# P·V of the last two token tiles from float16 halves: splitting softmax weights and v, with the subtraction shared by VectorE and GpSimd

## The chip, the cores and the metric

The kernel runs on one core of a Trainium2 chip. The metric is the device time of one execution in microseconds (us); lower is better. The core has a matrix engine (TensorE, PE in the profile, with its weight loads listed apart as PEld), VectorE (DVE), ScalarE (ACT), GpSimd (POOL) and SyncE (SP), which issues most DMAs. Each engine works through its own queue in the order in which the program stands there, and waits on semaphores of the others. PSUM, where matmul results land, is short here: two one-bank tiles for dense products (m0, m1), two two-bank tiles for scores (s) and one two-bank tile (po).

## The reference

The input x is 2048 tokens of 512 numbers. The output is x + s * g: s is sliding-window attention over a layer-normed x, g a gated feed-forward branch of x that goes through one more SiLU.

```python
H = 32; Dh = D // H; W = 256                                   # D = 512, so Dh = 16
qkv = (x @ wqkv).reshape(B, S, 3, H, Dh).transpose(2, 0, 3, 1, 4)
scores = jnp.einsum("bhqd,bhkd->bhqk", q, k) * (Dh ** -0.5)
mask = (idx[:, None] - idx[None, :] >= 0) & (idx[:, None] - idx[None, :] < W)
p = softmax(where(mask, scores, -1e9)); o = jnp.einsum("bhqk,bhkd->bhqd", p, v)   # then @ wo
gate = x @ w1; up = x @ w3; h = silu(gate) * up; out = h @ w2                    # F = 1792
xn = layernorm(x); s = A(xn, wqkv, wo); g = silu(B(xn, w1, w3, w2)); return x + s * g
```

All is float32 in the reference. A query sees itself and the 255 keys before it.

## The kernel before

**Halves.** Nearly every product is float32 made of float16 halves: a number a is split into hi = float16(a) and lo = float16(a - hi), and three matmuls hi·hi, hi·lo and lo·hi are summed in PSUM. ScalarE usually writes hi and VectorE or GpSimd writes lo as a subtraction. One product is not split: the softmax weights times v (called P·V here) is a float32 matmul.

**Units.** Tokens come in four tiles of 512 (t = 0 to 3) and heads in four groups of eight (g). A unit is a pair of heads in each half of the group (p = 0, 1), so there are 32 units, numbered n = 8t + 2g + p. A unit has a first pass (`pass1`, L653: row maxima of the scores, which VectorE takes at L685) that runs two units ahead, and a second pass (`pass2`, L738): scores again, transposed, with the maximum subtracted (L759), masks added on VectorE (L766), exponential on ScalarE into a float32 tile pt of 128x1024 (L769), and then P·V (L787).

The second pass of a unit is cut into five chunks c0 to c4 of scores for t > 0 (`CHUNKS`). Chunk c0 is for both heads a; c1 and c3 are for a = 0, c2 and c4 for a = 1. P·V takes 48 matmuls per unit: the array is used as eight tiles of 64 rows by 32 columns, so eight matmuls (two row halves h, four heads) run side by side. `values` (L773) puts them in six such groups of eight: the first is of c0, the next two of c1 and c2, the last three of c3 and c4. The columns that one array tile takes in the six groups are 256, 320, 192, 320, 128 and 64 (or 64 and 128): 1280 in all. V holds 16 columns of v and a column of ones for each head, so that the sum of the weights comes out of the same matmul.

**Order.** The PE queue is in the order of the text (`ORDERED`); on the other engines a scheduler decides, and work under `urgent()` goes ahead. A unit's work on PE is written as five batches (`PLAN`, in `batches`) with dense matmuls between them (`spread`): W stands for a chunk of scores, M, X and N for a piece of the first pass of the unit after next, and the last batch holds P·V. Before, c0, c1 and c2 come in the first three batches and c3 with c4 in the fourth; the first pass of the last batch is 16 narrow matmuls (48 rows by 32 columns), right ahead of P·V. The last two units, which have no first pass beside them, go by `LAST_PLANS` with four batches.

**Dense work** between the batches is the feed-forward branch (`gate_up`, L1055; `folds`, L1198, a seven-product scheme for the down projection at t > 1), the projections (`project`, L601, and `value`, L567) and the output product (`total`, L1332). For t > 1, VectorE's product at L1079 makes one 128x512 float32 tile h of the feed-forward branch. Two such tiles make the operands of the folded product: `fold_first` (L1115, four operations on GpSimd, L1121 to L1113) after the first, `fold_second` (L1127, eleven, L1136 to L1113) after the second. `turn_beside` (L504) transposes the normed x of a later token tile beside the scores; it costs VectorE two copies of 128x256 for each piece (L524, L525).

**Buffers.** pt tiles are five float32 buffers. Other temporary tiles are taken from 54 slots of 2 KB per partition (`take`, `give`).

## Time and profile before

| | |
|---|---|
| median of three runs | 804.23 us (804.05 to 804.49) |
| the profiled execution | 803.54 us, of which its span on the core is 801.4 us |
| busy: PE, DVE, ACT, POOL | 791.6, 620.4, 395.5, 387.6 us |
| P·V on PE (L787) | 77.2 us in 2880 instructions |
| granted clock of PE | full |

A float32 matmul stands in the trace as two matmuls and two weight loads, so the 1440 matmuls of P·V are 2880 rows. A busy PE has its pipeline filled; a row's duration has the time through the array in it, so that starts, and not durations, tell the rate. "Idle before" is time in which the engine had nothing running. The times of the views that follow are counted from the start of the span.

### The profile page before, as it was taken

How to read it: one execution, taken by the hardware profiler on the slowest of the kernel's cores; microseconds unless marked ns; L12 is line 12 of the kernel's file. 1: busy time of each engine (PE TensorE's matmuls, PEld its weight loads, DVE VectorE, ACT ScalarE, POOL GpSimd, SP SyncE). 2: the span in 40 equal slices, each digit the busy share in tenths (PEclk: the TensorE clock that was granted, in tenths of full speed). 3: DMA queues.
4: the chain of work that ended last, by engine and by line, in shares of the span. 5: the costliest groups of instructions: out<-in, count | busy, mean ns of one | idle time of the engine just before them, and what ended most of it. 6: DMA issues, size and time to landing. Idle time of an engine off the chain costs nothing.

```text
span 801.4 us, 23995 instructions
## 1 busy us (share of the span) xinstructions
PE 791.6 (99%) x9181; PEld 404.0 (50%) x9181; DVE 620.4 (77%) x2001; ACT 395.5 (49%) x596; POOL 387.6 (48%) x762
## 2 busy tenths in 40 slices
PE   9999999999999999999999999999999999999997
PEld 4444445444454444444445444466544744467465
DVE  8886889778798678787888887776678876874537
ACT  6989777744355544344443344344434334444411
POOL 2357657633329436365443546330446276650770
PEclk9999999999999999999999999999999999999999
DMA  9887655636666564657556743656553553343431
GB/s 284 239 260 239 202 185 145 242 111 193 189 216 187 168 212 139 212 156 255 142 191 171 209 115 101 180 169 159 140 158 90 156 161 106 89 121 127 133 89 60
DMA packets 109858, 134.18 MB, mean 167 GB/s; under 512 B 18928, under 2 KB 64944, under 8 KB 109744
## 3 DMA queue, kind: packets, MB, share of 16 engines
q1 hardware_dynamic: 109456, 132.13, 55.4%
q8 instruction: 72, 1.18, 0.7%
q10 hardware_dynamic: 288, 0.52, 0.2%
q14 instruction: 42, 0.34, 0.1%
HBM read 91.23 MB, written 36.57 MB: 159 GB/s over the span
## 4 chain that ended last, share of the span: by engine, by line
PE 81%; DVE 6%; DMA 5%; ACT 3%; SPq 3%; issue 1%; POOL 1%; DVEq 0%; ACTq 0%; POOLq 0%
PE m L1055 31%; PE po L787 9%; PE m L601 8%; PE m L1198 8%; PE m L1280 7%; PE s L759 5%; PE m L1332 4%; PE m L567 4%; PE s L671 3%; DMA slot<-in_B_w_dram 2%; PE po L671 2%; DVE junk L685 1%; POOL slot L345 1%; DMA KA<-dK 1%; SPq L880 1%
## 5 line engine op out<-in xcount | busy, mean ns | idle before, releaser
L1055 PE MATMUL m<-XH,slot 128*128 128x512 f16 x896 | 267.3, 380 | 0.8 <-DVE slot L1074 0.4
L769 ACT ACTIVATE pt<-s,es 128x1024 f32<-128x1024 f32 x152 | 167.6, 1113 | 175.9 <-DVE s L766 168.8
L1055 PEld LDWEIGHTS <-slot 128*128 128x128 f16 x1344 | 124.8, 98 | 155.2 <-issue 12.6
L1055 PE MATMUL m<-XL,slot 128*128 128x512 f16 x448 | 169.8, 379 | 0.0
L766 DVE TENSOR_TENSOR s<-s,MK 128x256 f32<-128x256 f32 (+2 forms) x280 | 118.8, 434 | 54.5 <-PE s L759 50.0
L685 DVE CUSTOM_DVE_ANT_0 junk<-s,MW 128x320 bf16<-128x320 f32 x276 | 133.9, 485 | 19.8 <-PE s L671 11.3
L339 POOL TENSOR_TENSOR slot<-slot,slot 128x256 f16<-128x256 f32 (+1 forms) x86 | 57.6, 693 | 121.4 <-DVE slot L1336 54.7
L345 POOL TENSOR_TENSOR slot<-slot,slot 128x128 f16<-128x128 f32 x184 | 74.9, 441 | 77.8 <-ACT slot L343 51.3
L685 DVE CUSTOM_DVE_ANT_0 junk<-po,MW 128x320 bf16<-128x320 f32 x172 | 83.4, 485 | 4.6
L1280 PE MATMUL m<-slot,slot 128*128 128x512 f16 x336 | 78.5, 380 | 1.4 <-DVE slot L1074 1.4
L787 PE MATMUL po<-pt,V 64*32 64x320 f32 (+4 forms) x2880 | 77.2, 342 | 0.1
L601 PE MATMUL m<-XH,slot 128*128 128x512 f16 x240 | 70.8, 380 | 0.5 <-DVE slot L1074 0.5
L1198 PE MATMUL m<-slot,slot 128*128 128x256 f16 x588 | 68.4, 273 | 0.0
L1070 ACT ACTIVATE slot<-m,sgs 128x512 f32<-128x512 f32 x56 | 38.3, 685 | 60.4 <-PE m L1055 60.3
L1113 POOL TENSOR_TENSOR slot<-slot,slot 128x256 f16<-128x256 f32 x98 | 64.6, 671 | 1.1
L1198 PEld LDWEIGHTS <-slot 128*128 128x128 f16 x588 | 56.2, 98 | 11.4 <-issue 2.8
L787 PEld LDWEIGHTS po<-pt,V 64*32 64x32 f32 x2880 | 50.5, 106 | 22.4 <-issue 0.8
L1074 DVE SCALAR_TENSOR_TENSOR slot<-slot,m 128x512 f32<-128x512 f32 x56 | 38.3, 684 | 28.4 <-ACT slot L1070 27.9
L759 PE MATMUL s<-qa,KA 50*64 50x320 f16 (+3 forms) x1472 | 58.3, 259 | 0.0
L601 PEld LDWEIGHTS <-slot 128*128 128x128 f16 x392 | 36.5, 98 | 42.6 <-issue 1.8
L759 PEld LDWEIGHTS <-KA 50*64 50x64 f16 x1472 | 30.1, 105 | 51.7 <-issue 31.5
L1280 PEld LDWEIGHTS <-slot 128*128 128x128 f16 x336 | 30.8, 98 | 39.5 <-issue 5.1
(194 smaller groups left out, 1132.6 us busy)
## 6 DMA issues: line engine op xcount, KB each, us to landing
slot<-dW SPq DMA_DIRECT2D x98, 256.0 KB
slot<-in_B_w_dram SPq DMA_DIRECT2D x56, 256.0 KB
slot<-dFold SPq DMA_DIRECT2D x48, 256.0 KB
dW<-slot SPq DMA_DIRECT2D x42, 256.0 KB
slot<-in_A_x_dram SPq DMA_DIRECT2D x30, 256.0 KB
KA<-dK SPq DMA_DIRECT2D x24, 288.0 KB
slot<-dWQ SPq DMA_DIRECT2D x24, 256.0 KB
qa<-dQ SPq DMA_DIRECT2D x30, 192.0 KB
```

Source lines behind the costliest of these rows:

```text
L339: op(out[:, c], a[:, c], b[:, c])
L345: nc.gpsimd.tensor_sub(lo[:, c:c + P], raw[:, c:c + P], hi[:, c:c + P])
L601: nc.tensor.matmul(cell["pp"][:, cols[n]], w[:, (a * NC + c) * P:(a * NC + c + 1) * P], b[:, c, cols[n]], start=n == 0 and (c, i) == parts ...
L685: lasts["maximum"] = nc.vector.tensor_tensor_reduce(out=junk[:, :n], in0=s[:, r, :n], in1=mask, scale=1.0, scalar=NEG, op0=ALU.add, op1=AL ...
L759: nc.tensor.matmul(s[64 * h:64 * h + 64, r, o:o + 64 * n], ka[rows, 2 * p + a, 64 * (m + 4):64 * (m + 5)], qa[rows, 2 * p + a, 64 * (m + k ...
L766: nc.vector.tensor_add(v, v, MK[:, kind, of:of + n, :].unsqueeze(1).to_broadcast([P, 2 * len(which), n, 64]))
L769: lasts["exp"] = nc.scalar.activation(pt, s, AF.Exp, scale=es)
L787: nc.tensor.matmul(cell["po"][32 * i:32 * i + 32, h, 64 * (m + k):64 * (m + k + n)], V[64 * h:64 * h + 64, (4 * t + m // 2) % VB, hd * VW: ...
L1055: nc.tensor.matmul(cell[k], w[:, (a * NC + c) * P:(a * NC + c + 1) * P], b[:, c, :], start=c == 0 and i == 0, stop=c == NC - 1 and i == 2)
L1113: nc.gpsimd.tensor_sub(lo, view, hi)
L1198: nc.tensor.matmul(cell["ps"][:, c], made[:, f:f + P], wj[:, g:g + 256], start=j == j0 and c == 0 and n == 0, stop=j == j1 - 1 and n == 2, ...
L1280: nc.tensor.matmul(ps, hh[:, a * TW + b * P:a * TW + (b + 1) * P], w[:, c * D:(c + 1) * D], start=f == f0 and i == 0, stop=f == f1 - 1 and ...
```

## The change

Four things, in neutral words:

1. For t > 1 (units 16 to 31) P·V is made of three float16 matmuls in place of one float32 matmul: hi of v times hi of p, lo of v times hi of p, hi of v times lo of p, group by group, each pass of eight matmuls after the other (L825). After the exponential, ScalarE copies pt to float16 (L801), and lo = pt - hi is made in three pieces: columns 512 to 1023 on VectorE (L802) and two of 256 on GpSimd (L804). The float32 pt tile has two buffers by turns there; hi and lo of c0 and c1 lie in slots, those of c2, c3 and c4 in one buffer each.
2. v comes as float16 halves for blocks 8 to 15: hi by ScalarE, lo by VectorE (L586), with four small memsets on GpSimd each. Blocks 6 and 7 are split on their own (`part_values`) in unit 13. v is scaled by a constant now, where before a number worked out from the weights was used; two small VectorE operations on that number go away.
3. For units 16 to 29 the batches are dealt out differently (`PARTED_PLAN`): c0 and c1 share the first batch and c2, c3 and c4 have a batch each, with two pieces of the first pass beside each of them. `parted` lets finishing a maximum and `turn_beside` follow each other in neighbouring pieces.
4. `measure` for feed-forward blocks 4 and 5 (t = 0) has two of its four squares on VectorE instead of ScalarE. The output product of the very last block goes in column parts of 256, 128 and 128 instead of 256 and 256.

```diff
@@ value
-            if half:
+            if not half:
+                return
+            by_head = lambda v: v[:, 0:H * VW].rearrange("p (h w) -> p h w", w=VW)
+            pv = pv.rearrange("p (h d) -> p h d", d=DH)
+            s = VS / (WS * XS)
+            if j < 8:
                 with urgent():
-                    nc.scalar.activation(V[:, j % VB, 0:H * VW].rearrange(...)[:, :, 0:DH], pv.rearrange(...), AF.Copy, scale=sc["uv"])
+                    nc.scalar.activation(by_head(V[:, j % VB, :])[:, :, 0:DH], pv, AF.Copy, scale=s)
+                return
+            both = V[:, j % VB, :].bitcast(F16)
+            VF[j] = hi, lo = both[:, 0:VR], both[:, VR:]
+            with urgent():
+                nc.scalar.activation(by_head(hi)[:, :, 0:DH], pv, AF.Copy, scale=s)
+                lasts["emptied"] = nc.vector.scalar_tensor_tensor(by_head(lo)[:, :, 0:DH], pv, s, by_head(hi)[:, :, 0:DH],
+                                                                  op0=ALU.mult, op1=ALU.subtract)
+            for v, one in ((hi, VS / OS), (lo, 0.0)):
+                nc.gpsimd.memset(by_head(v)[:, :, DH], one)
+                nc.gpsimd.memset(v[:, H * VW:], 0.0)
@@ pass1
-            elif alone[0] and maxima and (ii, a) != (0, 0):
+            elif alone[0] and maxima and (parted[0] or (ii, a) != (0, 0)):
...
-            alone[0] = not after or t * NG + g <= 2
+            alone[0] = not after or t * NG + g <= 2 or parted[0]
@@ pass2, scores
-            cell[c] = pt = ppool.tile([P, 2, 512], F32, name="pt")
+            pt = ppool.tile([P, 2, 512], F32, name="pt", tag=f"pt{c % 2 if t > 1 else in_pt[0] % 5}", bufs=1)
             with urgent():
                 lasts["exp"] = nc.scalar.activation(pt, s, AF.Exp, scale=es)
+            if t < 2:
+                cell[c] = pt
+                return
+            if c < 2:
+                cell[c] = hi, lo = [take(F16) for _ in range(2)]
+            else:
+                both = ppool.tile([P, 2048], F16, name="pt", tag=f"pt{c}", bufs=1)
+                cell[c] = hi, lo = both[:, 0:1024], both[:, 1024:]
+            pt = pt.rearrange("p r q -> p (r q)")
+            with urgent():
+                lasts["exp"] = nc.scalar.copy(hi, pt)
+                nc.vector.tensor_sub(lo[:, 512:], pt[:, 512:], hi[:, 512:])
+                for q in (0, 256):
+                    nc.gpsimd.tensor_sub(lo[:, q:q + 256], pt[:, q:q + 256], hi[:, q:q + 256])
@@ pass2, values
+            groups = list(zip_longest(*(turns[k] for k in sorted(turns))))
+            if t > 1:
+                for group in groups:
+                    for kv, kp in ((0, 0), (1, 0), (0, 1)):
+                        for c, o, h, a, (m, k, n, _, _) in filter(None, group):
+                            for r in range(2):
+                                ...
+                                nc.tensor.matmul(cell["po"][32 * i:32 * i + 32, h, 64 * (m + k):64 * (m + k + n)],
+                                                 VF[4 * t + m // 2][kv][64 * h:64 * h + 64, hd * VW:hd * VW + 32],
+                                                 cell[c][kp][64 * h:64 * h + 64, 512 * r + o:512 * r + o + 64 * n], ...)
+                give(*cell[0], *cell[1], after=2)
+                return
@@ measure
-        sb = squares([...], on_act=4 if f > 2 else 2, apart=apart)
+        sb = squares([...], on_act=4 if f > 4 else 2, apart=apart)
@@ total_by_columns
-        for c in (slice(0, 256), slice(256, 512)):
-            ps = bank([P, 256])
+        for c in (slice(0, 256), slice(256, 384), slice(384, 512)):
+            ps = bank([P, c.stop - c.start])
@@ plans
     PLAN = (("WM", ()), ("WMX", ()), ("WMX", ()), ("WWX", ()), ("NN", (0, 1, 2, 3, 4)))
+    PARTED_PLAN = (("WW", ()), ("WMX", ()), ("WMX", ()), ("WMX", ()), ("NN", (0, 1, 2, 3, 4)))
-        plan = AHEAD_PLAN if not u else LAST_PLANS[n - len(units) + 2] if not ahead else PLAN if u[0] else FIRST_PLAN
+        plan = AHEAD_PLAN if not u else LAST_PLANS[n - len(units) + 2] if not ahead else (FIRST_PLAN, PLAN, PARTED_PLAN, PARTED_PLAN)[u[0]]
@@ part_values (new)
+        for j in (6, 7):
+            VF[j] = hi, lo = [take(F16) for _ in range(2)]
+            with behind_exp():
+                nc.scalar.copy(hi[:, 0:VR], V[:, j, :])
+            for c in range(0, VR, 256):
+                cols = slice(c, min(c + 256, VR))
+                nc.gpsimd.tensor_sub(lo[:, cols], V[:, j, cols], hi[:, cols])
```

How the queues move is shown at three places.

On PE, the end of unit 18: the last of the narrow matmuls of the first pass and the start of P·V. Before, eight float32 matmuls of one group are one row each, and no weight load stands apart:

```order
L671 LDWEIGHTS qa
L671 MATMUL s<-KA_141,qa 32x320
L787 MATMUL po<-pt,V 32x256 x8
L787 MATMUL po<-pt,V 32x320 x8
L787 MATMUL po<-pt,V 32x192 x8
L787 MATMUL po<-pt,V 32x320 x8
L787 MATMUL po<-pt,V 32x128 x4
L787 MATMUL po<-pt,V 32x64 x8
L787 MATMUL po<-pt,V 32x128 x4
```

In the changed kernel the first group of the same unit reads (V and slot_6329 are the halves of v, slot_8544 and slot_8545 hi and lo of c0; each kind stands several times):

```order
L690 LDWEIGHTS qa
L690 MATMUL s<-KA_141,qa 32x320
L825 LDWEIGHTS V
L825 MATMUL po<-slot_8544,V 32x256
L825 LDWEIGHTS slot_6329
L825 MATMUL po<-slot_8544,slot_6329 32x256
L825 LDWEIGHTS V
L825 MATMUL po<-slot_8545,V 32x256
L825 LDWEIGHTS V
L825 MATMUL po<-slot_8563,V 32x320
```

48 instructions have become 144 matmuls with a weight load each, and the lo half of a chunk is read in the third pass of a group.

On GpSimd, unit 31. Before, `fold_first` of one pair of tiles and `fold_second` of it follow each other:

```order
L1121 TENSOR_TENSOR slot_13235<-slot_13214 128x256
L1112 CAST slot_13234<-slot_13235 128x256
L1113 TENSOR_TENSOR slot_13234<-slot_13214,slot_13234 128x256
L1113 TENSOR_TENSOR slot_13234<-slot_13235,slot_13234 128x256
L1136 TENSOR_TENSOR slot_13311<-slot_13214,slot_13289 128x256
L1137 TENSOR_TENSOR slot_13311<-slot_13311,slot_13214 128x256
L1113 TENSOR_TENSOR slot_13315<-slot_13289,slot_13315 128x256
L1138 TENSOR_TENSOR slot_13235<-slot_13289,slot_13311 128x256
L1113 TENSOR_TENSOR slot_13315<-slot_13289,slot_13315 128x256
L1112 CAST slot_13344<-slot_13311 128x256 x2
L1113 TENSOR_TENSOR slot_13344<-slot_13311,slot_13344 128x256 x2
L1112 CAST slot_13224<-slot_13235 128x256
```

In the changed kernel the same pair, from the last operations of `fold_first` on (L804 x4 is lo of c2 and c3, the last row lo of c4):

```order
L1164 TENSOR_TENSOR slot_15139<-slot_15140,slot_15139 128x256
L804 TENSOR_TENSOR pt<-pt 128x256 x4
L1187 TENSOR_TENSOR slot_15226<-slot_15119,slot_15204 128x256
L1188 TENSOR_TENSOR slot_15226<-slot_15226,slot_15119 128x256
L1164 TENSOR_TENSOR slot_15230<-slot_15204,slot_15230 128x256
L1189 TENSOR_TENSOR slot_15140<-slot_15204,slot_15226 128x256
L1163 CAST slot_15264<-slot_15226 128x256 x2
L1164 TENSOR_TENSOR slot_15264<-slot_15226,slot_15264 128x256 x2
L1163 CAST slot_15129<-slot_15140 128x256
L1164 TENSOR_TENSOR slot_15129<-slot_15140,slot_15129 128x256
L804 TENSOR_TENSOR pt<-pt 128x256 x2
```

Lo of c2 and c3 stands between the two, and lo of c4 behind the whole of `fold_second`. The same order (all of `fold_second`, then lo of c4) is found in units 17 and 26; in unit 28 seven of the eleven operations stand ahead of it.

On VectorE, unit 16, the third batch (c3 in the changed kernel). Before:

```order
L766 TENSOR_TENSOR s<-s,MK 128x2x2x64
L685 ISA junk,M<-s,MW 128x320
L524 CAST XH<-s 128x2x128
L685 ISA junk,M<-po,MW 128x320
L525 TENSOR_TENSOR XL<-s,XH 128x2x128
L1079 SCALAR_TENSOR_TENSOR slot_7555<-m_7606,slot_7555 128x512
```

Now:

```order
L785 TENSOR_TENSOR s<-s,MK 128x2x2x64
L704 ISA junk,M<-s,MW 128x320
L529 CAST XH<-s 128x2x128
L704 ISA junk,M<-po,MW 128x320
L530 TENSOR_TENSOR XL<-s,XH 128x2x128
L802 TENSOR_TENSOR pt<-pt 128x512
L529 CAST XH<-po 128x2x128
L1130 SCALAR_TENSOR_TENSOR slot_7616<-m_7684,slot_7616 128x512
L530 TENSOR_TENSOR XL<-po,XH 128x2x128
```

A subtraction of the softmax weights and a second piece of `turn_beside` have come in. Over the whole unit VectorE has ten copies of `turn_beside` (L529, L530) where it had four, over unit 17 six as before, and over unit 18 none where it had six.

More of the change, by code (lines that the diff above doesn't have):

```diff
@@ L781, in values @@
                         turns.setdefault(item[1:3], []).append((c, *item))
-            for group in zip_longest(*(turns[k] for k in sorted(turns))):
+            groups = list(zip_longest(*(turns[k] for k in sorted(turns))))
[4 more added lines that the diff above has]
+                            for r in range(2):
+                                i = 2 * r + a
+                                hd = g * 8 + r * 4 + 2 * p + a
+                                nc.tensor.matmul(cell["po"][32 * i:32 * i + 32, h, 64 * (m + k):64 * (m + k + n)],
+                                                 VF[4 * t + m // 2][kv][64 * h:64 * h + 64, hd * VW:hd * VW + 32],
+                                                 cell[c][kp][64 * h:64 * h + 64, 512 * r + o:512 * r + o + 64 * n],
+                                                 start=(h, i) not in begun, stop=c == len(chunks) - 1 and kp == 1,
+                                                 skip_group_check=True)
+                                begun.add((h, i))
+                give(*cell[0], *cell[1], after=2)
+                return
+            for group in groups:
                 for c, o, h, a, (m, k, n, _, _) in filter(None, group):
@@ L1492, in batch @@
                 alone[0] = True
+                parted[0] = bool(u) and u[0] > 1
                 for f in rows:
@@ L1652, in tile_block @@
             second()
+        if n == 13:
+            later(2, part_values)
         if n == 6:
@@ L1657, in tile_block @@
             beside_scores(12, lambda s: then(s, wout[2](s), lambda: later(2, lambda: wout[3](2)), lambda: later(3, out_scale)))
+        if n == 24:
+            later(1, lambda: give(*VF.pop(6), *VF.pop(7)))
         want += a_unit - other[n]
```

18 lines of the change are left out of this document (11 added, 7 removed).

## The prediction

> **What bounds the kernel now.** I read the page's head first, then its chain of waits and its groups of instructions.
>
> ```profile
> PE 791.6 (99%) x9181; PEld 404.0 (50%) x9181; DVE 620.4 (77%) x2001; ACT 395.5 (49%) x596; POOL 387.6 (48%) x762
> PE 81%; DVE 6%; DMA 5%; ACT 3%; SPq 3%; issue 1%; POOL 1%; DVEq 0%; ACTq 0%; POOLq 0%
> L787 PE MATMUL po<-pt,V 64*32 64x320 f32 (+4 forms) x2880 | 77.2, 342 | 0.1
> ```
>
> TensorE is busy 99% of the span and carries 81% of the chain that ended last; ahead of P·V (L787) it idled 0.1 us in the whole run. Time is therefore saved only where the PE queue gets shorter, and any new wait in that queue is paid in full, because nothing idle stands behind it to give it back. A row's duration has the way through the array in it, so I take starts from PE's timeline; these are around one P·V, and one dense stretch of the chain.
>
> ```profile
> 562.55 0.64 PE L759 MATMUL s<-qa,KA 50*64 50x320 f16 x24
> 563.02 0.31 PE L671 MATMUL po<-KA,qa 48*64 48x320 f16 x4
> 567.28 0.47 PE L671 MATMUL s<-KA,qa 48*32 48x320 f16 x16
> 567.56 2.53 PE L787 MATMUL po<-pt,V 64*32 64x256 f32 x96
> 570.03 0.60 PE L1055 MATMUL m<-XH,slot 128*128 128x512 f16 x2
> 448.02 3.99 PE m L1055 x18
> ```
>
> P·V of a unit occupies 570.03 - 567.56 = 2.47 us. The dense stretch gives the streaming rate: 3.99 us / (18 x 512) = 0.43 ns per column.
>
> **P·V on PE.** An array tile takes 1280 columns. Two rows per float32 matmul at 2.47 us fit four passes over them: 4 x 1280 x 0.43 = 2.20 us, and some 0.3 us of change-over (2.17 with the unrounded rate). Three float16 passes stream in 1.63 us; with the same 0.3 a unit takes 1.92, a gain of 0.55 us, over 16 units **-8.8 us**. The bounds: with the change-over mostly gone 1.74 us, -11.6 in all. On the other side, what may count is not columns but pairs of load and matmul: there are 144 now against 96. The trace has 24 pairs in 563.02 - 562.55 = 0.47 us (19.6 ns each) and 16 in 567.56 - 567.28 = 0.28 (17.5). 144 at 19.6 ns are 2.82 us, +0.35 a unit, **+5.7** in all. I take the streaming end: both those stretches carry enough columns to be at the streaming rate themselves (16 x 320 over eight tiles x 0.43 = 0.28), so they are no evidence of a floor per pair.
>
> The Trainium skill, "TensorE: Matmul & The Clock Gate", section "Wait — 56ns, not 53.3ns?", says that starts never come closer than about 25 ns however small the matmul is. By that rule 144 would take 3.6 us and the change would lose some 18 us on PE alone, an estimate from that page. The trace disagrees with it for matmuls on separate array tiles: 17.5 ns.
>
> **The new work beside it.** 80 chunks pass through it, five in each of 16 units. Durations by kind, from the groups kept apart by shape:
>
> ```profile
> L769 ACT ACTIVATE pt<-s,es 128x1024 f32<-128x1024 f32 x152 | 167.6, 1113 | 175.9 <-DVE s L766 168.8 <-DVE M L685 3.0 <-PE m L1280 2.3
> L343 ACT CAST slot<-slot 128x512 f16<-128x512 f32 x46 | 27.4, 610 | 0.5
> L1110 ACT CAST slot<-slot 128x256 f16<-128x256 f32 x42 | 15.6, 403 | 59.8 <-DVE slot L1079 59.8
> L766 DVE TENSOR_TENSOR s<-s,MK 128x256 f32<-128x256 f32 x224 | 92.9, 427 | 54.1 <-PE s L759 49.8 <-ACT slot L1088 1.4 <-PE s L711 0.9
> L1338 DVE TENSOR_TENSOR slot<-slot,slot 128x512 f32<-128x512 f32 x3 | 2.0, 683 | 0.0
> L524 DVE CAST XH<-s 128x256 f16<-128x256 f32 x17 | 7.1, 420 | 0.0
> L1113 POOL TENSOR_TENSOR slot<-slot,slot 128x256 f16<-128x256 f32 x98 | 64.6, 671 | 1.1
> ```
>
> ScalarE's copy of 1024 columns: 256 more cost 207 ns, so 610 + 2 x 207 = 1.03 us. VectorE's subtraction 0.68, GpSimd's two 1.30 to 1.34. A unit gains 5.2 us on ScalarE, 3.4 on VectorE, 6.6 on GpSimd, in a period of some 23 us. On average there is room on all three; what decides is the place in the queue. The halves of v (eight short VectorE operations, and `part_values` in unit 13) fall where ScalarE and GpSimd have room; I cost them at nothing beyond VectorE's share below.
>
> When is c4 wanted? Take T4 as the start of its scores on PE. Ahead of P·V stand c4's scores (0.24), two pieces of the first pass (0.3), 18 dense matmuls (3.99) and the 16 narrow ones (0.28): P·V starts at T4 + 4.8. The first lo of c4 is read behind the first three groups and two passes of the fourth: (3 x 768 + 2 x 320) columns x 0.43 = 1.25 us later, at **T4 + 6.1**. It is ready after 0.24 of scores, two masks (0.87), the exponential (1.11), the copy (1.03), some 0.25 of hand-overs, so hi at T4 + 3.5, and 1.3 on GpSimd: **T4 + 4.8**. The spare is 1.3 us in a unit in which GpSimd is free. It is not free where `fold_second` stands ahead of c4's lo in its queue, as in units 17, 26, 31 and for seven of eleven operations 28. GpSimd and PE there:
>
> ```profile
> 451.56 0.73 POOL L1136 TENSOR_TENSOR slot<-slot,slot 128x256 f32<-128x256 f32 x1 [8.92 <-DVE slot L1079]
> 458.03 0.73 POOL L1121 TENSOR_TENSOR slot<-slot 128x256 f32<-128x256 f32 x1
> 451.94 0.64 PE L759 MATMUL s<-qa,KA 50*64 50x320 f16 x24
> ...
> 652.43 0.73 POOL L1136 TENSOR_TENSOR slot<-slot,slot 128x256 f32<-128x256 f32 x1 [4.09 <-DVE slot L1079]
> 651.55 0.64 PE L759 MATMUL s<-qa,KA 50*64 50x320 f16 x24
> ...
> 698.00 0.73 POOL L1136 TENSOR_TENSOR slot<-slot,slot 128x256 f32<-128x256 f32 x1 [3.25 <-DVE slot L1079]
> 696.67 0.64 PE L759 MATMUL s<-qa,KA 50*64 50x320 f16 x24
> ...
> 748.77 0.73 POOL L1136 TENSOR_TENSOR slot<-slot,slot 128x256 f32<-128x256 f32 x1
> 756.38 1.30 POOL L1113 TENSOR_TENSOR slot<-slot,slot 128x256 f16<-128x256 f32 x2
> 760.43 0.73 POOL L1136 TENSOR_TENSOR slot<-slot,slot 128x256 f32<-128x256 f32 x1 [2.75 <-DVE slot L1079]
> 765.19 2.55 PE L787 MATMUL po<-pt,V 64*32 64x256 f32 x96
> ```
>
> `fold_second` lasts 458.03 - 451.56 = 6.47 us and starts when VectorE's second product lands. Unit 17: start near T4 (it was 0.4 before; c3's lo now stands ahead), so c4's lo is done at T4 + 0.1 + 6.5 + 1.3 = 7.9, **+1.8**. Unit 26: product at 652.43 = T4 + 0.9, lo at T4 + 8.65, **+2.5**. Unit 28: T4 + 1.3, 4.6 us of it ahead, lo at T4 + 7.2, a wait of 1.1; with lo of the earlier chunks still in the queue up to 3.1; I take **+2**. Unit 31: GpSimd had the previous `fold_second` and a `fold_first` from 748.77 to 757.68. With 2.6 us for lo of c0 and c1 these end at 760.3, with c2 and c3 at 762.9, then `fold_second` to 769.4, c4's lo at 770.7. P·V, 0.55 us shorter in each unit alike, would want it at 765.19 - 0.55 + 1.25 = 765.9: **+4.8**. Together **+11.1**. Behind the waiting matmul everything on PE waits.
>
> **The common price of VectorE and GpSimd.** A VectorE subtraction with both inputs in SBUF is new here at this density. The opening shows such a meeting:
>
> ```profile
> L345 POOL TENSOR_TENSOR slot<-slot,slot x184: 416/428/907, 31.7 to 245.9; 128x128 f16<-128x128 f32 x184
> 31.69 2.42 POOL L345 TENSOR_TENSOR slot<-slot,slot 128x128 f16<-128x128 f32 x5 [26.40 <-DMA dQ<-slot]
> 31.84 0.82 DVE L251 CUSTOM_DVE_ANT_0 junk<-slot 128x512 bf16<-128x512 f32 x1
> L251 DVE CUSTOM_DVE_ANT_0 junk<-slot 128x512 bf16<-128x512 f32 x10 | 7.0, 698 | 0.1
> ```
>
> GpSimd's subtractions range from 0.43 to 0.91 us, the first five take 2.42 where 5 x 0.43 = 2.14 were due, and VectorE's square beside them 0.82 instead of 0.70. So an overlap costs up to 0.48 us on GpSimd. In ordinary units the spare of 1.3 us covers it; in the four units above it is paid, 4 x 0.5 = **+2**. The Trainium skill, "SBUF — State Buffer", section "Who interferes with whom", calls this an exclusive lock in which the later operation waits out the whole earlier one. By it the four units pay 0.7 each, an estimate; the row shows less.
>
> **VectorE near its limit.** Stretches of one unit, P·V to P·V:
>
> ```profile
> core 0: us, PE busy (x) PEld busy (x) DVE busy (x) ACT busy (x) POOL busy (x), PEclk, DMA share, GB/s
> 368.10:388.70 20.60, 20.60 (x271) 9.67 (x256) 19.65 (x61) 10.12 (x14) 11.96 (x20) 1.00 0.69 199
> 410.90:433.90 23.00, 23.00 (x312) 11.18 (x297) 20.35 (x59) 9.53 (x13) 13.21 (x23) 1.00 0.53 154
> ```
>
> The last is unit 16. It gets 3.4 of subtractions and six more copies of `turn_beside` (6 x 0.42 = 2.5): 20.35 + 5.9 = 26.3 us of work in 23.0. If all the excess were paid it would be +3.3, but what isn't urgent slides into units 17 and 18, which lose copies. 19.65 in 20.60 (the first row) was carried without any wait of PE. Between 0 and 3.3 I take **+2.5**, near the upper end, since masks, maxima and the subtraction there are all awaited.
>
> **The end and the squares.** The last column part has 128 columns instead of 256, so VectorE's two last operations shrink:
>
> ```profile
> L1369 DVE SCALAR_TENSOR_TENSOR slot<-m,us,slot 128x256 f32<-128x256 f32 x2 | 1.0, 482 | 0.2 <-PE m L1367 0.2
> L1370 DVE TENSOR_TENSOR slot<-slot,slot 128x256 f32<-128x256 f32 x2 | 0.9, 426 | 0.1
> ```
>
> They come after the last matmul; halved widths save about **-0.2**. Two squares moved per pair of blocks cost VectorE 0.70 each and relieve ScalarE as much, in stretches where neither is waited for: nothing; if VectorE is awaited there, +1.4.
>
> **The sum**, on the profiled execution (803.54): -8.8 + 11.1 + 2 + 2.5 - 0.2 = +6.6, 810.1. The median of the runs is 0.7 above that execution: **811 us**.
>
> **The rivals.** *(1) The waits don't come; only the matmuls get shorter.* For it: on average the three engines have room, and each of my waits hangs on `fold_second` starting where it did; if VectorE's product lands 2 us earlier against c4's scores, units 17, 26 and 28 wait for nothing. Against it: GpSimd's queue is in order, and unit 31 is a sum of work without a gap. Time: 803.5 - 8.8 + about 1.5 + 0.7 = 797; 794 with the -11.6. *(2) Pairs, not columns, set the pace of P·V.* At 19.6 ns: +5.7 in place of -8.8; c4's lo is then wanted 0.5 us later, so four waits lose 2: 803.5 + 5.7 + 9.1 + 4.3 + 0.7 = 823. It decides above 17 ns, where 144 pairs take the 2.47 us of before. *(3) The meeting of the two engines costs more than I take*, so that ordinary units use up their 1.3 us as well: 0.7 for VectorE's subtraction ahead and 0.5 on each of two pieces exceed it by 0.4; in twelve units that is +5, 816, and with waits of VectorE in its turn 820. *(4) Gains and waits cancel*, with the four waits at half: 804.
>
> **How the numbers follow.** Main case 0.52, (1) 0.30, (2) 0.06, (3) 0.08, (4) 0.04. A measurement of this kernel can tell about 0.2%, 1.6 us, from no change. Slower takes all of (2) and (3) and most of the main case, whose own range is 804 to 817: 0.62; the same 0.05; faster 0.33, (1) with the lowest part of the main case. The range of 8 in 10 reaches from the body of (1) to that of (3): 796 to 820.
>
> **What would show it.** P·V at 1.9 us from its start to the next matmul in a unit without waits, at 2.5 or more if (2) holds. Idle PE ahead of the third pass of the fourth group in units 17, 26, 28 and 31, released by GpSimd, 1.8, 2.5, 2 and 4.8 us; if these are missing, (1). GpSimd's lo pieces at 0.67 us, and up to 1.1 where VectorE subtracts beside them. VectorE busy over 95% in unit 16. I am wrong at once if lo of c4 is done before the fourth group wants it in unit 31, or if idle time before P·V has VectorE or ScalarE as its releaser in most units.

## The result and the profile after

The changed kernel takes 888.23 us (887.52 to 888.33) beside 804.22 for the kernel before: the ratio is 1.104, with a 95% interval of 1.102 to 1.106. I had forecast slower, 811 us, and a range up to 820. The sign held; the size was wrong by a factor of twelve, 84 us in place of 7.

First the page of the changed kernel: busy time of the engines, and the groups of the new subtractions (L804 on GpSimd, L802 on VectorE).

```profile
PE 811.9 (92%) x9961; PEld 414.2 (47%) x9961; DVE 704.2 (80%) x2093; ACT 469.7 (53%) x674; POOL 532.3 (60%) x960
L804 POOL TENSOR_TENSOR pt<-pt 128x256 f16<-128x256 f32 x96 | 78.3, 838 | 49.1 <-ACT pt L801 39.0
L802 DVE TENSOR_TENSOR pt<-pt 128x512 f16<-128x512 f32 x48 | 47.2, 983 | 31.6 <-ACT pt L801 31.5
L802 DVE TENSOR_TENSOR slot<-pt,slot 128x512 f16<-128x512 f32 x32 | 32.0, 1003 | 32.7 <-ACT slot L801 32.7
```

TensorE was busy 99% of the span and is now busy 92% of a longer one. Two readings lie in the last three rows. VectorE's subtraction has a mean of 0.98 to 1.00 us where 0.68 was expected, GpSimd's piece 0.84 where 0.67 was expected. And VectorE stood idle 31.6 + 32.7 = 64 us ahead of its subtractions, because ScalarE's copy was not done.

The list of what TensorE waited for (total, times, longest) shows that no single wait took over:

```profile
PE po L825 <- POOL pt L804: 16.3, 11, 4.1
PE s L690 <- ACT pt L790: 9.1, 15, 2.2
PE m L1106 <- DVE slot L1125: 9.0, 6, 3.8
PE s L778 <- DVE M L704: 7.8, 11, 1.4
PE po L690 <- DVE XL L530: 4.9, 3, 2.8
PE m L620 <- DVE slot L1130: 2.8, 1, 2.8
```

The first row is the wait I had predicted, P·V for lo of a chunk from GpSimd, though in 11 places and not in four. The others are waits for which I had nothing but the +2.5 us of VectorE in unit 16: a scores bank that the exponential frees too late, a dense bank that VectorE empties too late, maxima that come too late.

P·V itself did what was computed. In unit 16, where it waited for nothing, these are its first instructions and the first matmul behind it:

```profile
442.92 0.27 PE L825 MATMUL po<-slot,V 64*32 64x256 f16 x1
444.85 0.82 PE L1331 MATMUL m<-slot,slot 128*128 128x512 f16 x3
```

444.85 - 442.92 = 1.93 us; the prediction said 1.92, and before it was 2.46. The 16 units gained 8.5 us there.

Per unit, from one P·V to the next, a row of the view by stretches tells how the load stands (us, then busy time and instructions of PE, PEld, DVE, ACT, POOL, then the granted clock and the share and rate of DMA). The stretches are units 15 to 16, 16 to 17 and 25 to 26:

```profile
core 0: us, PE busy (x) PEld busy (x) DVE busy (x) ACT busy (x) POOL busy (x), PEclk, DMA share, GB/s
412.25:442.92 30.67, 26.11 (x360) 12.68 (x347) 26.43 (x70) 15.53 (x20) 23.18 (x41) 0.94 0.49 142
442.92:472.25 29.33, 26.05 (x377) 12.56 (x361) 23.78 (x64) 13.25 (x16) 17.96 (x27) 0.88 0.30 79
683.54:711.16 27.62, 23.98 (x347) 12.84 (x324) 22.43 (x59) 11.35 (x14) 20.42 (x28) 0.94 0.47 134
```

Every unit of the changed half has grown, by 1.0 to 7.6 us, and no engine is full in most of them: in the last row VectorE is busy 22.4 of 27.6 us, GpSimd 20.4, ScalarE 11.4. The engines wait for each other, as the list above shows for TensorE. The first row is unit 16, for which I had expected VectorE to be busy over 95% and 2.5 us to be lost: VectorE was busy 26.43 of 30.67 us, 86%, and 7.6 us were lost against the 23.03 of before. The granted clock fell to 0.88 and 0.94 in such stretches, where it had been 1.00 throughout; the last section says what that costs.

### The profile page after: what moved, and what is told of

It reads as the page before. It is cut to its first block, busy times and chain, and to the rows that moved or that the text cites. A ratio compares the mean times of both kernels' runs of the same rounds, so it can differ in the third digit from the quotient of the medians.

```text
span 885.7 us, 26000 instructions
## 1 busy us (share of the span) xinstructions
PE 811.9 (92%) x9961; PEld 414.2 (47%) x9961; DVE 704.2 (80%) x2093; ACT 469.7 (53%) x674; POOL 532.3 (60%) x960
## 5 line engine op out<-in xcount | busy, mean ns | idle before, releaser
L1106 PE MATMUL m<-XH,slot 128*128 128x512 f16 x896 | 273.1, 387 | 11.8 <-DVE slot L1125 9.0
L1106 PEld LDWEIGHTS <-slot 128*128 128x128 f16 x1344 | 127.3, 99 | 170.5 <-issue 31.1
L1106 PE MATMUL m<-XL,slot 128*128 128x512 f16 x448 | 172.6, 385 | 0.0
L804 POOL TENSOR_TENSOR pt<-pt 128x256 f16<-128x256 f32 x96 | 78.3, 838 | 49.1 <-ACT pt L801 39.0
L620 PE MATMUL m<-XH,slot 128*128 128x512 f16 x240 | 73.7, 393 | 5.5 <-DVE slot L1130 2.8
L1164 POOL TENSOR_TENSOR slot<-slot,slot 128x256 f16<-128x256 f32 x98 | 72.1, 750 | 1.0
L802 DVE TENSOR_TENSOR pt<-pt 128x512 f16<-128x512 f32 x48 | 47.2, 983 | 31.6 <-ACT pt L801 31.5
L804 POOL TENSOR_TENSOR slot<-pt,slot 128x256 f16<-128x256 f32 x64 | 48.9, 789 | 37.8 <-ACT slot L801 37.8
L1249 PEld LDWEIGHTS <-slot 128*128 128x128 f16 x588 | 56.3, 98 | 13.2 <-issue 4.3
L620 PEld LDWEIGHTS <-slot 128*128 128x128 f16 x392 | 37.4, 100 | 50.8 <-issue 10.5
L802 DVE TENSOR_TENSOR slot<-pt,slot 128x512 f16<-128x512 f32 x32 | 32.0, 1003 | 32.7 <-ACT slot L801 32.7
```

The costliest lines, as they stand in the source:

```text
L620: nc.tensor.matmul(cell["pp"][:, cols[n]], w[:, (a * NC + c) * P:(a * NC + c + 1) * P], b[:, c, cols[n]], start=n == 0 and (c, i) == parts ...
L802: nc.vector.tensor_sub(lo[:, 512:], pt[:, 512:], hi[:, 512:])
L804: nc.gpsimd.tensor_sub(lo[:, q:q + 256], pt[:, q:q + 256], hi[:, q:q + 256])
L1106: nc.tensor.matmul(cell[k], w[:, (a * NC + c) * P:(a * NC + c + 1) * P], b[:, c, :], start=c == 0 and i == 0, stop=c == NC - 1 and i == 2)
L1164: nc.gpsimd.tensor_sub(lo, view, hi)
L1249: nc.tensor.matmul(cell["ps"][:, c], made[:, f:f + P], wj[:, g:g + 256], start=j == j0 and c == 0 and n == 0, stop=j == j1 - 1 and n == 2, ...
```

## The experiments

The theories. **A**: the subtractions lose the time, by themselves or because VectorE and GpSimd block each other. **B**: the other order of the batches, or the copy on ScalarE, does. Later ones: **C**, the copy makes ScalarE's queue late; **D**, a waiting subtraction at the head of VectorE's queue holds up what stands behind it; **E**, the new order of the batches makes those queues late; **F**, the amount of work; **G**, too few float32 buffers. The edits are against the changed kernel if nothing else is said; the ratios are against the kernel before. A scheduler orders every queue but that of PE, so an operation left out could reorder the rest. It hardly did in the runs without a part of the subtractions: the subtractions aside, VectorE's operations from 410 us on follow each other as in the changed kernel to 98% or more.

### Subtractions: none, GpSimd's alone, VectorE's alone

```diff
-                nc.vector.tensor_sub(lo[:, 512:], pt[:, 512:], hi[:, 512:])
-                for q in (0, 256):
-                    nc.gpsimd.tensor_sub(lo[:, q:q + 256], pt[:, q:q + 256], hi[:, q:q + 256])
...
-                                                 cell[c][kp][64 * h:64 * h + 64, ...],
+                                                 cell[c][0][64 * h:64 * h + 64, ...],
```

> The changed kernel without any subtraction; the third pass of P·V reads hi where lo stood, so TensorE and ScalarE have the same work and lo of the softmax weights is left out of the result. Theory A (the subtractions lose the 84 us: by their length, and by the blocking of VectorE and GpSimd while both read two operands from SBUF): about 797 us (804.2 - 8.8 for the shorter P·V, + 1.4 that the trace of the changed kernel had already lost at unit 15). Theory B (the copy on ScalarE, or the other order of the batches, delays the chunks): it stays above 840.

Measured: **821.6 us** (ratio 1.021, 1.019 to 1.022), between the two expectations. Some 66 us hang on the subtractions, but 24 more than expected remain without any.

The second run keeps GpSimd's lines alone, with `cell[c][kp * (1 - r)]`, the third VectorE's alone, with `cell[c][kp * r]`.

> The changed kernel with GpSimd's two subtractions alone; VectorE has none, and the third pass reads hi in place of lo for columns 512 to 1023, so half of lo is left out. Theory A1 (VectorE and GpSimd block each other): far less than half of the loss remains, 800 to 812 us, the upper end if the waits behind fold_second that I predicted (11 us) are there by themselves. Theory A2 (GpSimd's queue is simply too long, 13 more us of work every two units): over 840.

Measured: **845.9 us** (1.051, 1.048 to 1.053).

> The changed kernel with VectorE's subtraction alone; GpSimd has none, the third pass reads hi in place of lo for columns 0 to 511. Theory A1: a VectorE subtraction now meets only the GpSimd operations of before: 798 to 812 us. Theory A3 (VectorE is the full engine, 3.4 us a unit too much): over 830. If the two halves cost little each and 84 together, the loss is in their meeting.

Measured: **851.9 us** (1.057, 1.054 to 1.061). So GpSimd's half costs 845.9 - 821.6 = 24.3 us, VectorE's half 30.3, and both together 66.6: each is dear by itself, and having both adds 66.6 - 24.3 - 30.3 = 12 us, of which some 6 are the slower clock (an estimate of the last section) and the rest can be their meeting. Theory A1, that the loss is mainly the meeting, falls. The numbers expected for A2 (over 840) and A3 (over 830) were met, but that doesn't show a full engine: VectorE is busy 80% of the span in its run, GpSimd 59% in its own.

In the run with GpSimd's half alone the predicted wait stands free of the others. GpSimd and PE at the end of unit 26 (the numbers are start and duration; L803 is lo of c3, then of c4, L1186 to L1163 `fold_second`):

```profile
674.98 1.30 POOL L803 TENSOR_TENSOR pt<-pt 128x256 f16<-128x256 f32 x2 [3.70 <-ACT pt L801]
676.24 0.73 POOL L1186 TENSOR_TENSOR slot<-slot,slot 128x256 f32<-128x256 f32 x1
...
682.71 1.30 POOL L803 TENSOR_TENSOR pt<-pt 128x256 f16<-128x256 f32 x2
684.06 0.73 PE L824 MATMUL po<-pt,V 64*32 64x320 f16 x54 [3.42 <-POOL pt L803]
```

`fold_second` runs from 676.24 to 682.71, its 6.47 us, lo of c4 follows, and TensorE waits 3.42 us in the middle of P·V.

### The order of the batches

P·V and v in float32 as before, all the rest of the change kept:

```diff
-            if t > 1:
+            if False:
                 for group in groups:
                     for kv, kp in ((0, 0), (1, 0), (0, 1)):
...
-            if j < 8:
+            if True:
                 with urgent():
                     nc.scalar.activation(by_head(V[:, j % VB, :])[:, :, 0:DH], pv, AF.Copy, scale=s)
```

> The changed kernel with P·V and v in float32 as before: what is left of the change is the order of the batches (PARTED_PLAN), the constant scale of v, the two squares on VectorE and the three column parts. Theories A: 803 to 807 us. Theory B in its second form (the order of the batches loses the time): over 830.

Measured: **806.2 us** (1.002, 1.001 to 1.003). From P·V of unit 15 to that of unit 16 it took 25.14 us against 23.03, which is as much as the whole difference: there VectorE has the six more copies of `turn_beside`. The other stretches differ by -0.7 to +0.9 us and cancel, so squares and column parts can't be told apart from scatter.

The reverse, the changed kernel with the batches of before:

```diff
-(FIRST_PLAN, PLAN, PARTED_PLAN, PARTED_PLAN)[u[0]]
+(FIRST_PLAN, PLAN, PLAN, PLAN)[u[0]]
-                parted[0] = bool(u) and u[0] > 1
+                parted[0] = False
```

> The changed kernel with the batches of before (c0, c1 and c2 in one batch each, c3 with c4 in the fourth) and maxima finished as before. With float32 P·V the new order cost 1.9 us. Theory E (the new order, with two chunks at once at a unit's start, makes the queues of ScalarE and GpSimd late): 860 or less. If the order serves the new P·V: above 888, since c4 then comes as late as before and together with c3, 1.3 us of GpSimd and 1.0 of ScalarE more ahead of its lo.

Measured: **883.7 us** (1.099, 1.097 to 1.101). Neither expectation was met: the order hardly matters, and what there is of it speaks against the new one.

### The copy on ScalarE

The exponential writes the float16 tile itself:

```diff
-                lasts["exp"] = nc.scalar.activation(pt, s, AF.Exp, scale=es)
...
-                lasts["exp"] = nc.scalar.copy(hi, pt)
+                lasts["exp"] = nc.scalar.activation(hi.rearrange("p (r q) -> p r q", r=2), s, AF.Exp, scale=es)
```

> The changed kernel without subtractions and without ScalarE's copy: the exponential writes the float16 tile itself, and TensorE still makes three passes (the third reads hi; lo of the softmax weights is left out). The run without subtractions alone came at 821.6. Theory C (the copy makes ScalarE's queue later: exponentials, and the activations that empty the two dense PSUM banks, come later, and TensorE waits for a bank): 797 to 801, which is the 806.2 of the float32 P·V in the new order less 8.7. Theory B2 (the three-pass P·V or its v halves lose the time): it stays near 820.

Measured: **807.4 us** (1.004, 1.002 to 1.005). The copy costs 821.6 - 807.4 = 14.2 us on an engine that is busy 57% of the time: theory C. How an engine with so much room delays TensorE is seen in the run without subtractions. ScalarE, VectorE and PE in unit 20 to 21:

```profile
537.43 2.12 ACT L790 ACTIVATE pt<-s,es 128x1024 f32<-128x1024 f32 x2 [2.06 <-DVE s L785]
539.43 1.99 ACT L801 CAST slot<-pt 128x1024 f16<-128x1024 f32 x2
541.32 0.61 ACT L637 ACTIVATE slot<-m 128x512 f16<-128x512 f32 x1
541.96 0.69 DVE L641 SCALAR_TENSOR_TENSOR slot<-m,slot 128x512 f16<-128x512 f32 x1 [3.77 <-ACT slot L637]
542.70 0.38 PE L572 MATMUL m<-wvh,XH 128*128 128x512 f16 x1 [0.90 <-DVE slot L641]
```

Two exponentials and two copies, 4 us, stand ahead of the small operation L637 that reads a dense PSUM bank. VectorE's L641, which empties the bank, waits 3.77 us for it with everything behind it; then TensorE waits for the bank.

The 807.4 is still 9.7 us above 806.2 - 8.5. Part of it are waits of TensorE for which the profile shows no releaser. The two longest lie in the middle of the scores and in the middle of P·V:

```profile
642.10 0.24 PE L778 MATMUL s<-qa,KA 50*64 50x192 f16 x1 [1.81 <-issue]
731.15 0.23 PE L820 MATMUL po<-pt,V 64*32 64x128 f16 x2 [1.45 <-issue]
```

The page's count for "issue" on these lines is 4.2 us in that run, and none in the next one, which has 768 PE rows fewer. My guess is the supply of instructions. No run tests it, but the traces speak for it: they hold DMA packets of 16 KB on a queue of the kind "instruction", and one of them ends 1.6 us before TensorE goes on at the first place (639.02 to 640.52) and 1.3 us before it at the second (728.51 to 729.88). The two other idle times of this kind over 0.3 us in this run, and all eleven in the three runs of the section on subtractions, likewise end 1.0 to 1.5 us after such a packet.

Set beside the float32 run unit by unit, nearly all of the 9.7 us has a place. The stretch to P·V of unit 26 is 3.7 us longer than the shorter P·V allows: the first of these waits, and behind it 3.4 us in which the granted clock was 0.50. The other three waits lengthen three units by 3.0 us together. Units 14 and 16, longer in every run with v's halves, have 0.9, unit 21 has 1.3 (with a wait of 0.8 for the transfer dWQ), and 0.9 lie ahead of unit 14, within the scatter there. So the halves of v themselves cost about 0.9 us, and "issue" with the clock behind it 6.7.

### Two passes instead of three

```diff
-                    for kv, kp in ((0, 0), (1, 0), (0, 1)):
+                    for kv, kp in ((0, 0), (1, 0)):
```

> As the run without copy, but with two passes only (hi and lo of v, each times the float16 softmax weights; lo of the weights is left out). If P·V is paced by columns, a unit loses one pass of 1280 columns at 0.42 ns, 0.54 us, in all 8.6 us less than the run without copy (so 788 to 793); if by pairs, 48 x 13 ns = 0.62 us a unit, 10 us less.

Measured: **796.9 us** (0.992, 0.989 to 0.995; its runs scatter from 794.6 to 801.3), 10.5 us less than with three passes. P·V of a unit takes 1.34 us, 0.59 less than 1.93, so 9.4 us of it are P·V, between the price by columns (0.54) and by pairs (0.62). The "issue" waits of 4.2 us went away as well with the half clock behind them, and a transfer (dWQ) was waited for 3.7 us instead of 0.8.

### What costs the time in VectorE's half

```diff
-                nc.vector.tensor_sub(lo[:, 512:], pt[:, 512:], hi[:, 512:])
-                for q in (0, 256):
-                    nc.gpsimd.tensor_sub(...)
+                mx = small.tile([P, 1], F32, name="mx")
+                nc.vector.tensor_reduce(mx, hi[:, 512:], mybir.AxisListType.X, ALU.max)
```

> As the run with VectorE's subtraction alone (851.9), with the subtraction replaced by a maximum over the same 512 columns of hi: the same wait for ScalarE's copy at the same place in VectorE's queue, about the same length, but one operand in SBUF instead of two. lo is left out of the result. Theory D (a wait at the head of VectorE's queue and 3.4 us more work a unit lose the time): within 8 us of 852. Theory A1 (the meeting with GpSimd's operations does): near the 822 of no subtraction.

Measured: **843.6 us** (1.050, 1.048 to 1.053). Here are the durations (min/median/max) and the idle time before the operation, first with the subtraction, then with the maximum:

```profile
L802 DVE TENSOR_TENSOR pt<-pt x48: 681/693/1203, 428.0 to 812.9; 128x512 f16<-128x512 f32 x48
  ACT slot L801: 31.0, 27
  ACT pt L801: 26.3, 40
```

```profile
L803 DVE TENSOR_REDUCE mx<-pt x48: 675/686/689, 428.3 to 804.4; 128x1 f32<-128x512 f16 x48
  ACT slot L801: 33.9, 31
  ACT pt L801: 26.0, 40
```

The operation with one operand in SBUF (of float16, where the subtraction reads one of float32 and one of float16) never takes longer than 0.689 us, the one with two takes up to 1.203: that is the meeting with GpSimd, and with what follows from it it is worth 851.9 - 843.6 = 8.3 us. About half of that is the slower clock: at equal granted clock the runs of the two kernels lie 4 us apart (847.2 against 843.1 to 843.7 us at 0.998, 851.8 and 852.0 against 847.9 at 0.992). But 843.6 - 821.6 = 22 us are lost by an operation that is never lengthened. It waits as long at its place in the queue (60 us in all), and what stands behind it waits with it. Theory D takes the larger part, though 843.6 lies just outside its range.

### Repairs

VectorE's subtraction of a chunk is queued behind the masks of the next one (of c0 and c1 behind those of c2):

```diff
+            if c < 4:
+                kept.append(subtract)
...
+            if c != 1:
+                with tc.issue_after(mask.ins):
+                    while kept:
+                        kept.pop(0)()
```

> The changed kernel, all of its work kept, with VectorE's subtractions of c0 and c1 queued behind the masks of c2, that of c2 behind the masks of c3, that of c3 behind those of c4; GpSimd's as they were. Theory D (a subtraction waits for ScalarE's copy at the head of VectorE's queue, 64 us in the run of the change, while masks, maxima and the operations that empty PSUM banks stand behind it): 850 to 872, since those operations go first; VectorE's idle time ahead of the subtractions falls below 20 us. Theory F (VectorE and GpSimd are simply too full in sum): 880 to 892.

Measured: **868.3 us** (1.079, 1.077 to 1.082). VectorE's idle time ahead of its subtractions, with all the work kept:

```profile
  ACT pt L806: 6.6, 8
  ACT slot L806: 0.9, 1
```

7.5 us instead of 64, and 20 us of the time come back, by another place in the queue alone.

Three float32 buffers instead of two (`tag=f"pt{(0, 1, 'x')[c % 3] ...}"`, and `SLOTS = 52`):

> The changed kernel with three float32 buffers for pt by turns instead of two (and 52 slots instead of 54 for other tiles). Theory G (an exponential waits until GpSimd has read the buffer of two chunks before; ScalarE sat idle 26.6 us for that in the run of the change): 860 to 876. If that idle time lies beside other waits: 884 to 889.

Measured: **881.6 us** (1.096, 1.094 to 1.098). The idle time of ScalarE for a buffer fell from 26.6 to 1.4 us, and 6.6 us were won; the expectation for theory G was more, so most of that idle time lay beside other waits: P·V now waited 22.6 us for GpSimd where it had waited 16.3.

Lo of c4 wholly on VectorE:

```diff
+                if c == 4:
+                    nc.vector.tensor_sub(lo, pt, hi)
+                else:
```

> The changed kernel with the whole lo of c4 made by VectorE, so that no P·V waits for GpSimd's queue at its end. My predicted mechanism (lo of c4 behind fold_second): P·V's own waits, 21.6 us in the run of the change, fall to a few, 866 to 874 us with 0.6 us more of VectorE in each unit. If other waits take their place at once: 880 to 890.

Measured: **877.0 us** (1.091, 1.089 to 1.094). P·V waited for VectorE 2.1 us and no longer for GpSimd, but the banks that VectorE empties (L1128 there) held TensorE 11.4 us instead of 9.0, the scores banks 12.9 instead of 9.1. Part of the gain was turned into other waits.

The same question without VectorE's subtractions in the way: the run with GpSimd's half alone, less c4 (`if c < 4:` ahead of the loop, and `kp * (1 - r) * (c < 4)`).

> The run with GpSimd's subtractions alone (845.9), without those of c4: lo of c4 is left out as a whole, of c0 to c3 for columns 512 to 1023. My predicted mechanism (lo of c4 stands behind fold_second; P·V's own waits in that run add up to 11 us more than without subtractions): 832 to 836. If GpSimd's load on the other chunks is what counts: 840 or more, a fifth less of +24.

Measured: **834.6 us** (1.038, 1.036 to 1.040), 11.2 us below 845.9. Lo of c4 on GpSimd is worth as much as was predicted for its wait, though some 4 us of it are the slower clock (an estimate of the last section); the other 834.6 - 821.6 = 13 us of GpSimd's half are its load on c0 to c3.

All three repairs together:

> The changed kernel with all of its work and the three repairs together: VectorE's subtractions queued behind the masks of the next chunk, lo of c4 wholly on VectorE, three float32 buffers. If each removes its own waits: 888 - 20 - 11 - 7 = 850, 845 to 856. If they remove the same ones, and the amount of work on VectorE and GpSimd is the limit: 862 to 870.

Measured: **856.6 us** (1.065, 1.062 to 1.068), 31.6 below the changed kernel where the single gains add up to 37.8. They remove mostly different waits, and 52 us above the kernel before remain. Places in the queues and one buffer are thus a good third of the loss; by the estimate of the last section some 11 of the 31.6 us come by way of the clock. What makes up the 52 this run doesn't tell; the run without any subtraction, with the copy, already lies 17 us above the kernel before.

### What is faster than both

Two passes, with the batches of before:

> The run with two passes (float16 softmax weights, lo of them left out, hi and lo of v), which took 796.9, with the batches of before in units 16 to 29. In float32 the new order cost 1.9 us, nearly all in unit 15 to 16, where VectorE copies six more pieces of the transposed x. If that carries over: 794 to 796.

Measured: **794.9 us** (0.989, 0.987 to 0.991). And in all 32 units:

```diff
+            hi = ppool.tile([P, 1024], F16, name="pt", tag=f"pt{in_pt[0] % 8}", bufs=1)
...
-            if t > 1:
+            if True:
                 for group in groups:
```

> Two float16 passes in all 32 units (float16 softmax weights written by the exponential, hi and lo of v; lo of the weights left out), batches as before. Against the 794.9 of the same in units 16 to 31: units 8 to 15 gain 1.1 us each (2.46 to 1.34), units 0 to 7 about 0.9 each (1.99 to 1.1), together -16; v's halves of eight more blocks cost VectorE 0.7 each early on, where it is over 85% busy. Expected 779 to 786; if VectorE is awaited there, up to 790.

Measured: **790.4 us** (0.983, 0.981 to 0.984), 4.5 us less than in half of the units, where 9 to 16 were expected. TensorE is busy 764.3 of 789.2 us; its longest wait is a transfer:

```profile
PE m L1091 <- DMA slot<-dW: 4.5, 1, 4.5
```

A faster kernel asks for its operands sooner, and here that one came late; I didn't try to move it. This kernel leaves lo of the softmax weights out, so it isn't the same computation to the last bits: the changed kernel with all of its work was not brought below the time of before.

## Why the prediction was right in sign and wrong in size

In the prediction's own steps, with the runs' differences as prices; they add up, since each is a step from one kernel to the next (804.2 to 806.2, 807.4, 821.6, 845.9 and so on to 888.2), and in another order of steps they could be shared out differently:

| step of the prediction | predicted | measured |
|---|---|---|
| P·V in three float16 passes | -8.8 | -8.5 |
| order of the batches, squares, column parts | with VectorE's +2.5, and -0.2 | +2.0 |
| the rest of the run without copy | halves of v at 0 | +9.7: "issue" and clock 6.7, halves of v about 0.9 |
| copy on ScalarE | 0 | +14.2 |
| lo of c4 on GpSimd | +11.1, behind `fold_second` | +11.2 |
| GpSimd's other subtractions | 0 | +13.0 |
| a VectorE operation of that length and wait | in one unit, part of +2.5 | +22.0 |
| two operands in SBUF, VectorE's half alone | with the next row +2 | +8.3 |
| both halves together, beyond their sum | | +12.1 |

Each price holds the slower clock that its waits brought along. By the estimate of the last section that is about 4 of the 11.2, 5 of the 8.3 and 6 of the 12.1 us.

**What held.** The time of P·V, 1.93 us against 1.92: the 0.42 ns a column and the 0.3 us of change-over were the right price, and pairs of load and matmul set no pace. The 11 us behind `fold_second` held as a sum, and that is in part luck: place by place they did not. In the run with GpSimd's half alone P·V took longer than 1.93 by 1.9 us in unit 17 (1.8 was predicted), 3.7 in 26 (2.5), 2.0 in 28 (2), yet only 0.7 in unit 31 (4.8), and units 19, 24 and 29 had 1.3 to 2.1 that I hadn't looked for; 29 has most of that without any subtraction as well. So the four units have 8.3 us of the 11.1, and the 11.2 is made full by other units and by the clock.

**The step that failed** is this one: "On average there is room on all three; what decides is the place in the queue." The second half is right, and I used it for one queue only. GpSimd's got a walk through its order; for ScalarE and VectorE I compared busy time with the period and wrote nothing, but for unit 16. Of the 84 us, 14 + 22 us lie exactly there: a long copy, or a subtraction whose input is late, stands ahead of the small operation that empties one of two dense PSUM banks. The rows for this were at hand: the order in which VectorE's subtraction follows the masks directly, and a copy of 1.03 us that lies between the exponential and the subtraction.

**The blocking had the right size for one meeting and the wrong number of them.** I priced a meeting at 0.48 us, on GpSimd's side alone, and counted it in four units: +2. The size is about right: GpSimd's piece takes up to 1.196 us instead of 0.67, VectorE's subtraction 1.2 instead of 0.69. But both are released by the same copy, so that in 73 of the 80 chunks one of the two was lengthened, by 24 us of busy time in all on each engine. The Trainium skill's page "SBUF — State Buffer", section "Who interferes with whom", says that the later one waits out the earlier; I read the opening's rows as milder. Here the added time is 0.50 us where 0.65 us of the other's recorded operation was left: a wait of the kind that the page tells of, at the price of the opening's row.

**Rival (3)** named the mechanism of ordinary units and put it at 820 at most, because it, too, priced the lock alone. Rival (1) fell with the first look at the waits, rival (2) with P·V's 1.93 us.

## What to carry to other kernels

Where an order is fixed ahead of time, price a new operation by what stands behind it in its queue while its input is late, on each engine it touches, and not by the engine's average room: 80 operations of 0.69 us on an engine with a fifth of its time free cost 22 us. Splitting an operand only pays if the split costs less than the matmuls it saves: here 8.5 us of matmul were bought with a copy and three subtractions for each chunk, which cost 81 us (14.2 + 11.2 + 13.0 + 22.0 + 8.3 + 12.1). Two operations that are released by one event and lengthen each other will meet nearly every time, here in 73 of 80 chunks.

## What was unexpected of the hardware

**VectorE held up through seven GpSimd operations.** One subtraction of the changed kernel, what GpSimd did in that time, and what came of it on VectorE and on PE:

```profile
664.49 4.42 DVE L802 TENSOR_TENSOR slot<-pt,slot 128x512 f16<-128x512 f32 x1 [0.94 <-ACT slot L801]
664.47 0.69 POOL L1164 TENSOR_TENSOR slot<-slot,slot 128x256 f16<-128x256 f32 x1
665.09 0.76 POOL L908 CAST slot<-on 128x256 f16<-128x256 f32 x2
665.79 1.32 POOL L344 TENSOR_TENSOR slot<-on,slot 128x256 f16<-128x256 f32 x2
667.04 1.31 POOL L804 TENSOR_TENSOR slot<-pt,slot 128x256 f16<-128x256 f32 x2
668.83 0.68 DVE L1130 SCALAR_TENSOR_TENSOR slot<-m,slot 128x512 f32<-128x512 f32 x1
669.56 1.01 PE L620 MATMUL m<-XH,slot 128*128 128x512 f16 x2 [2.78 <-DVE slot L1130]
672.80 0.59 PE L620 MATMUL m<-XH,slot 128*128 128x512 f16 x2
```

4.42 us for an operation of 0.69: GpSimd ran seven operations back to back in that time, and the subtraction ended only after the last of them. None of the other 79 took more than 1.24 us, so they waited for one operation at most. Why this one didn't get its turn, the trace doesn't show.

**A waiting TensorE gets half the clock for a while.** In the same rows, a pair of matmuls takes 1.01 us after the 2.78 us of idleness, and 0.59 from 672.80 on, 3 us later. The granted clock shows it; these are three such stretches (us, PE busy and its instructions, the granted clock, then share and rate of DMA):

```profile
429.88:433.30 3.42, 3.42 (x9) 0.50 0.64 231
464.02:470.84 6.82, 6.04 (x18) 0.50 0.29 57
668.82:672.23 3.41, 2.67 (x7) 0.50 0.20 75
```

The changed kernel has nine of them, eight of 3.4 us and one of 6.8; the kernel before has none. Each begins during a wait of TensorE or within 1.1 us of its end. The length of that wait alone doesn't decide: waits of 1.6, 1.5 and 1.4 us, with shorter ones near them, had a stretch soon behind them (the first of the three rows is one of these cases), while two of 2.5 us, at 524.64 and 838.19, had none. TensorE was busy 31.5 us in these stretches. If work at half the clock takes twice as long, they cost some 16 of the 84 us; this is an estimate, and the estimates of the clock's part above are made in the same way, from 3.4 us in the profile of the run without subtractions, 6.7 and 6.8 with GpSimd's and VectorE's alone, 3.1 without c4, 1.7 with the maximum and 4.9 with all repairs. The waits thus cost more than their own length, and this was in none of my terms.

**Pairs on separate array tiles have no floor near the old rate.** 144 float16 pairs in 1.93 us are 13.4 ns a pair, below the 17.5 that I had as the closest before, and P·V in two passes has 96 in 1.34, 14.0.
